# The value product of an attention stage issued in two parts, with its split into two float32r halves a step later

## The chip, the cores and the metric

One core of one Trainium2 chip runs the whole program. The metric is the device time of one execution in microseconds (us): 582.16 us for the kernel before, the median of three runs (581.98 to 582.57). The core has a matrix engine (TensorE, in the rows PE for its matmuls and PEld for its weight loads), a vector engine (VectorE, DVE), a scalar engine (ScalarE, ACT), a general one (GpSimd, POOL) and a queue that issues the DMAs (SyncE, SP). Each works through its own instructions in order and waits on semaphores for the others.

## The reference

A causal attention over 2 batches, 12 heads, 448 tokens and a head size of 64; its output, laid out as 896 tokens by 768, goes through two gated layers, all in float32.

```python
scores = where(causal mask, -1e9, q @ k.T / 8)
attn   = exp(scores - rowmax);  attn = attn / (rowsum + 1e-9)
x = (attn @ v), heads side by side             # 896 x 768
h = x @ w_in;  g = h * cos(h);  x = g @ w_out  # 2048 wide
out = ((x @ w_a) * (x @ w_b)) @ w_o2           # 1536 wide
```

## The kernel before

The kernel has an attention stage (the first 88 us) and four matrix products after it (`h`, `y`, `b` and `a`, `o` in the rows). The products run as float32r matmuls of 448 columns, each operand split into a high and a low half (`hi`, `lo`), three matmuls for one. The weights are unpacked and split on the fly: a chunk is loaded to `w_raw`, scaled on ACT (line 100), shifted, packed and signed on DVE (lines 105, 111, 118), and split on ACT or POOL (lines 129, 131, 138).

Attention works on pairs of heads, 12 in all (n = 0 to 11), four steps to a pair, 48 steps. The seven query blocks of 64 rows of a pair have score rows of 64 to 448 columns, packed into four PSUM banks (`BANKS`): {448}, {320, 192}, {384, 64}, {256, 128}; step 4n+b treats bank b. In each step the loop at line 515 goes through the table `CYCLE` and calls every function whose offset fits, so that the instructions stand on each engine in the order of the table, step by step. An entry with offset k belongs to pair n at step 4n+k. For one pair that means:

- `scores` (PE, line 339, tile `s`): 64x64 array tiles, every second step, two steps ahead, into four `s` banks in rotation. A bank can be refilled once `row_max` has read it.
- `row_max` (DVE, line 362, writes `p` and `mn`): mask, scale and row minimum; every step.
- `exps` (ACT, line 384): the exponentials and their row sums; every step.
- `recip` (DVE, lines 391 and 392, tile `sums`): steps 2 and 4. `scale_p` (POOL, line 399): steps 3 and 5.
- `transposes` (PE, line 413, tile `pt`): 7 full-array transposes at steps 5 and 7, into two `t` banks. `keep` (line 424 on ACT, 426 on DVE, tile `pp`): copies them to SBUF at steps 6 and 8, and so frees the banks.
- `values` (PE, line 440, tile `xa`): step 10, 14 matmuls (28 records, as a float32 matmul takes two passes) with 128x64 array tiles, of 384, 256, 128 and 64 columns.
- `x_hi` (ACT, line 450) at step 12 and `x_lo` (DVE, line 455) at step 13: the split of the result.

In the first four steps a dummy matmul (`warm`, line 460) follows each entry of `values` in the table. The weights of the first matrix product are treated in between by the table `ASIDE`: one chunk's scale at step 20, shift at 22, pack at 24, sign at 26, split on POOL at 28; the next ones from steps 32 and 46. From step 44 pieces of three matmuls of the product `h` are put in at the ends of steps.

Of the kernel before, what the change touches and what calls it, by code (L numbers as in the profile page):

```python
# [26 lines left out]
def tile_causal_attention_cos_gate_bilinear(  # L27
# [35 lines left out]
    def act_tiles(pool, tag, kind, b, n):  # L63
        return [
            tuple(pool.tile([P, S], F32R, tag=f"{tag}{b}_{t}{part}", name=f"{kind}{b}_{t}{part}") for part in ("hi", "lo"))
            for t in range(n)
        ]
# [89 lines left out]
    x = [act_tiles(xy, "xy", "x", b, NPAIR) for b in range(B)]  # L157
# [5 lines left out]
    def bank(tag, name):  # L163
        return psum.tile([P, 512], F32, tag=tag, name=name, bufs=BUFS[tag])

    def product(kind, f, acts, name, release, parts=1):

        ps = bank(next(cycle), name)[:, :S]
        n = len(acts)
        t = j = 0  # L170
        while t < n:
            hi, lo, k = chunks[kind, f, j]
            terms = [(hi, c, part) for c in range(k) for part in range(2)] + [(lo, c, 0) for c in range(k)]
            for i, (w, c, part) in enumerate(terms):
                nc.tensor.matmul(  # L175
                    ps,
                    w[:, c * P : (c + 1) * P],
                    acts[t + c][part],
                    start=t == 0 and i == 0,
                    stop=t + k == n and i == len(terms) - 1,  # L180
                )
                if (i + 1) % (len(terms) // parts) == 0 and i + 1 < len(terms):
                    yield ps
            t += k
            if release:
                del chunks[kind, f, j]
            if kind != "in":
                w_pump()
            j += 1
        yield ps  # L190
# [58 lines left out]
    NSTEP = NB * NP  # L249
# [10 lines left out]
    P_OFF, o = {}, 0  # L260
# [18 lines left out]
    with ExitStack() as actx:  # L279
        att = actx.enter_context(tc.tile_pool(name="att", bufs=2))  # L280
        T = {}
# [27 lines left out]
        @pairs  # L309
        def load_qk(n):  # L310
            b, i = divmod(n, NPAIR)
            T["raw", n] = t = att.tile([P, QK], F32, tag="qk_raw", name="qk_raw", bufs=4)
            cuts = (0, S + 2 * D, QK) if n == 0 else (0, QK)
            for c, d in zip(cuts, cuts[1:]):
                nc.sync.dma_start(out=t[:, c:d], in_=qk[b, i, :, c:d])

        @pairs
        def load_v(n):
            b, i = divmod(n, NPAIR)
            T["v", n] = t = att.tile([P, NJ, 2, D], F32, tag="v", name="v", bufs=4)  # L320
            nc.sync.dma_start(out=t, in_=v[b, i])

        @steps
        def scores(i):

            n, b = divmod(i, NB)
            if b % 2:
                return
            t = T["raw", n]
            for c in range(2):  # L330
                T["s", i + c] = bank("s", "s")
            for j in ORDER:
                c = 0 if j in BANKS[b] else 1
                if j not in BANKS[b + c]:
                    continue
                o = S_OFF[j]
                for e in range(2):
                    h, q = (slice(x * D, (x + 1) * D) for x in (e, SIDE[j][e]))
                    nc.tensor.matmul(  # L339
                        T["s", i + c][q, o : o + WIDTH[j]],  # L340
                        t[h, Q_COL[j] : Q_COL[j] + D],
                        t[h, FIRST[j] : FIRST[j] + WIDTH[j]],
                        start=True,
                        stop=True,
                    )
# [80 lines left out]
                    nc.vector.tensor_copy(dst, src)  # L426

        @pairs
        def values(n):

            T["xa", n] = ps = bank("x", "xa")
            pp, t = T["pp", n], T["v", n]

            parts = [(k, o, 6, pp[:, a:b]) for k, o, a, b in ((0, 0, 0, 3), (1, 2, 3, 5), (2, 4, 5, 6))]
            parts += [(3 + j // 2, TOKENS[j], TOKENS[j] + 1, pp[:, 6, j // 4]) for j in range(0, NJ, 2)]
            for k, o, w, p in parts:
                for e in range(2):
                    side = e if k < 3 else SIDE[2 * k - 6][e]
                    q = slice(side * D, (side + 1) * D)
                    nc.tensor.matmul(  # L440
                        ps[e * D : (e + 1) * D, o * D : w * D],
                        t[:, k, e],
                        p[:, :, :, q].rearrange("p s l q -> p (s l) q") if k < 3 else p[:, q],
                        start=k == 0,
                        stop=k == 6,
                    )
# [10 lines left out]
        def warm_up(n):  # L457
            ps = bank("x", "warm")
            for _ in range(n):
                nc.tensor.matmul(ps[:, :P], zeros, zeros, start=True, stop=True)  # L460
# [3 lines left out]
        def at(fn, i):  # L464

            n, b = divmod(i, NB)
            return i if fn in PER_STEP else n if b == 0 else -1
# [9 lines left out]
            (exps, 0),  # L477
            (scale_p, 3, 0),
            (scale_p, 5, 1),
            (values, 10),  # L480
            (transposes, 5, 0),
            (transposes, 7, 1),
            (x_hi, 12),
            (x_lo, 13),
            (load_qk, -10),
            (load_v, -2),
        ]
# [20 lines left out]
        with tc.manual_schedule():  # L508
            warm_up(7)
            load_qk(0)  # L510
            load_qk(1)
            load_qk(2)
            load_v(0)
            scores(0)
            for i in range(NSTEP + 14):
                for fn, offset, *args in CYCLE:
                    fn(at(fn, i - offset), *args)
                    if fn is values and i < WARM:
                        warm_up(1)
                for step, fn, *args in ASIDE:  # L520
                    if step == i:
                        fn(*args)
# [3 lines left out]
    with tc.manual_schedule():  # L526
# [20 lines left out]
        for m in range(N_Y):  # L547
            for b in range(B):
                ps = next(product("out", m, g[b], "y", b == B - 1))
# [15 lines left out]
        for m in range(N_Y):  # L565
            for b in range(B):
                ps = next(product("o2", m, c[b], "o", b == B - 1))
                o = work.tile([P, S], F32, tag="r", name="o")
# [50 lines left out]
```

## Time and profile before

| | |
|---|---|
| median of three runs | 582.16 us (581.98 to 582.57) |
| the profiled execution | 582.6 us, its span 580.5 us |
| granted TensorE clock | 1.00 of full speed |
| PE busy | 573.0 us, 99% |
| DVE, ACT, POOL busy | 361.7, 267.2, 222.9 us |
| attention | to 87.98 us |
| products | 87.98 us to the end |

The profile is of one execution. Its busy time of PE is modelled, since matmuls overlap, so the starts of the matmuls say more than the busy share. `x28` in a row is the number of records that were merged into it, `64*64` the array tile, and a bracket at the end of a row tells how long the engine had been idle and what released it.

### The profile page before, as it was taken

Reading aid. Unit: us, or ns where it says so; the run is one execution under the profiler, and the core shown is the slowest. Engines: PE = TensorE matmul, PEld = TensorE weight load, DVE = VectorE, ACT = ScalarE, POOL = GpSimd, SP = SyncE. Lnnn points to the kernel's source line nnn. Section 1 sums busy time; section 2 is a strip of 40 time slices with the busy share of each in tenths; the row PEclk is TensorE's granted clock in tenths of the full one; section 3 lists DMA queues with packets and bytes.
Section 4 is the critical chain, followed back from the end, with each engine's and each line's share of the span. In section 5 each row is a group of like instructions: output and inputs, shape, how many; then the busy total and the mean of one; then the engine's idle time right before and its main releaser. Section 6 shows DMA issues by size and latency. Waiting matters only on the chain.

```text
span 580.5 us, 8729 instructions
## 1 busy us (share of the span) xinstructions
PE 573.0 (99%) x3310; PEld 513.3 (88%) x3310; DVE 361.7 (62%) x599; ACT 267.2 (46%) x531; POOL 222.9 (38%) x200
## 2 busy tenths in 40 slices
PE   8999999999999999999999999999999999999997
PEld 6666679999999999999999999999999999999996
DVE  5888947777777765554455666666666666655400
ACT  5978937777777733232224333333333333222100
POOL 4567753666666643232223322222222222322200
PEclk9999999999999999999999999999999999999999
DMA  8755211333332343423243333333333333444000
GB/s 310 255 172 213 89 55 55 109 110 109 110 109 92 108 129 109 145 92 108 91 163 110 110 108 110 108 110 109 110 108 110 110 109 110 140 141 140 33 32 33
DMA packets 15450, 67.80 MB, mean 117 GB/s; under 512 B 1712, under 2 KB 3376, under 8 KB 15408
## 3 DMA queue, kind: packets, MB, share of 16 engines
q1 hardware_dynamic: 15408, 67.25, 34.4%
q8 instruction: 26, 0.43, 0.3%
q14 instruction: 16, 0.13, 0.1%
HBM read 64.49 MB, written 2.75 MB: 116 GB/s over the span
## 4 chain that ended last, share of the span: by engine, by line
PE 92%; DVE 3%; ACT 3%; issue 1%; POOL 0%; DVEq 0%; POOLq 0%
PE h L175 20%; PE y L175 20%; PE o L175 15%; PE a L175 15%; PE b L175 15%; PE xa L440 3%; ACT p L384 2%; PE pt L413 2%; PE s L339 2%; DVE p L362 1%; DVE pp L426 1%; PE warm L460 1%; ACT pp L424 0%; DVE sums L391 0%; DVE w_raw L118 0%
## 5 line engine op out<-in xcount | busy, mean ns | idle before, releaser
L138 POOL TENSOR_TENSOR w_lo<-w_raw,w_hi 128x768 fp32r<-128x768 f32 (+1 forms) x70 | 128.9, 1841 | 264.5 <-ACT w_hi L131 193.8
L111 DVE SCALAR_TENSOR_TENSOR w_raw<-w_raw 128x768 int32<-128x768 int32 (+1 forms) x70 | 124.4, 1778 | 63.3 <-ACT w_raw L100 62.4
L131 ACT ACTIVATE w_hi<-w_raw 128x768 fp32r<-128x768 f32 (+1 forms) x67 | 60.0, 896 | 163.1 <-DVE w_raw L118 99.9
L118 DVE SCALAR_TENSOR_TENSOR w_raw<-w_raw 128x768 int32<-128x768 int32 (+1 forms) x70 | 66.2, 946 | 0.4
L100 ACT ACTIVATE w_raw<-w_raw 128x768 f32<-128x768 f32 (+1 forms) x70 | 61.7, 881 | 0.0
L399 POOL TENSOR_SCALAR p<-p,sums 128x448 f32<-128x448 f32 (+6 forms) x84 | 44.0, 545 | 27.4 <-DVE sums L392 14.5
L384 ACT ACTIVATE p<-p,mn 128x448 f32<-128x448 f32 (+6 forms) x84 | 41.8, 501 | 13.4 <-DVE mn L362 13.2
L105 DVE TENSOR_SCALAR w_raw<-w_raw 128x768 int32<-128x768 int32 (+1 forms) x70 | 42.5, 607 | 0.0
L215 DVE SCALAR_TENSOR_TENSOR r<-k,h 128x448 f32<-128x448 int32 x32 | 19.8, 617 | 26.0 <-ACT k L214 25.7
L362 DVE CUSTOM_DVE_ANT_0 p<-s,mask 128x448 f32<-128x448 f32 (+6 forms) x84 | 31.3, 416 | 4.8 <-PE s L339 4.8
L569 DVE COPY o<-o 128x448 f32<-128x448 f32 x12 | 7.5, 624 | 35.3 <-PE o L175 35.3
L339 PE MATMUL s<-qk_raw 64*64 64x448 f32 (+6 forms) x336 | 28.1, 405 | 0.4 <-DVE mn L362 0.4
L214 ACT ACTIVATE k<-h 128x448 int32<-128x448 f32 x32 | 17.2, 538 | 18.4 <-PE h L175 17.6
L413 PE MATMUL pt<-ident,p 128*128 128x128 f32 x168 | 23.7, 279 | 1.9 <-ACT pp L424 1.2
L339 PEld LDWEIGHTS s<-qk_raw 64*64 64x64 f32 x336 | 15.9, 137 | 10.7 <-issue 3.9
L561 DVE TENSOR_TENSOR c<-a,bs 128x448 f32<-128x448 f32 x24 | 15.0, 624 | 15.3 <-PE a L175 15.3
L440 PEld LDWEIGHTS xa<-pp,v 128*64 128x64 f32 x336 | 16.1, 137 | 9.4 <-issue 7.1
L440 PE MATMUL xa<-pp,v 128*64 128x64 f32 (+3 forms) x336 | 23.8, 293 | 0.0
L413 PEld LDWEIGHTS pt<-ident,p 128*128 128x128 f32 x168 | 18.2, 141 | 4.8 <-issue 1.3
L231 DVE SCALAR_TENSOR_TENSOR r<-r,h 128x448 f32<-128x448 f32 x32 | 19.5, 609 | 1.5 <-ACT r L226 1.5
L221 ACT ACTIVATE r<-r 128x448 f32<-128x448 f32 x32 | 18.3, 571 | 0.0
L226 ACT ACTIVATE r<-r 128x448 f32<-128x448 f32 x32 | 18.2, 570 | 0.0
(377 smaller groups left out, 1564.6 us busy)
## 6 DMA issues: line engine op xcount, KB each, us to landing
w_raw<-in_w_in SPq DMA_DIRECT2D x16, 768.0 KB, 4.4
w_raw<-in_w_out SPq DMA_DIRECT2D x12, 768.0 KB, 4.3
w_raw<-in_w_b SPq DMA_DIRECT2D x12, 768.0 KB, 4.3
w_raw<-in_w_a SPq DMA_DIRECT2D x12, 768.0 KB, 4.3
w_raw<-in_w_o SPq DMA_DIRECT2D x12, 768.0 KB, 4.3
v<-in_v SPq DMA_DIRECT2D x12, 448.0 KB, 5.8
qk_raw<-in_qk SPq DMA_DIRECT2D x11, 448.0 KB, 5.6
w_raw<-in_w_out SPq DMA_DIRECT2D x6, 512.0 KB, 3.8
```

Of the source, the lines that this page charges most:

```text
L100: nc.scalar.activation(high, high, ACTF.Copy, scale=2.0**-112)
L105: nc.vector.tensor_single_scalar(low, low, 29, op=ALU.logical_shift_right)
L111: nc.vector.scalar_tensor_tensor(out=low, in0=high, scalar=3, in1=low, op0=ALU.logical_shift_left, op1=ALU.bitwise_or)
L118: nc.vector.scalar_tensor_tensor(out=low, in0=high, scalar=SIGN, in1=low, op0=ALU.bitwise_and, op1=ALU.bitwise_or)
L131: nc.scalar.activation(pair[0][:, :n], src, ACTF.Copy)
L138: engine.tensor_tensor(out=lo[:, :n], in0=f32(raw.pop(i)[:, :, 0]), in1=f32(hi)[:, :n], op=ALU.subtract)
L175: nc.tensor.matmul(ps, w[:, c * P : (c + 1) * P], acts[t + c][part], start=t == 0 and i == 0, stop=t + k == n and i == len(terms) - 1,)
L339: nc.tensor.matmul(T["s", i + c][q, o : o + WIDTH[j]], t[h, Q_COL[j] : Q_COL[j] + D], t[h, FIRST[j] : FIRST[j] + WIDTH[j]], start=True, st ...
L384: nc.scalar.activation(t, t, ACTF.Exp, bias=T["mn", n][:, c], scale=-1.0, accum_out=row_sum(n, j))
L399: nc.gpsimd.tensor_scalar(out=t, in0=t, scalar1=row_sum(n, j), scalar2=1.0, op0=ALU.mult, op1=ALU.mult)
L413: nc.tensor.transpose(dst, p_bufs[n % N_P][:, o : o + P], ident)
L440: nc.tensor.matmul(ps[e * D : (e + 1) * D, o * D : w * D], t[:, k, e], p[:, :, :, q].rearrange("p s l q -> p (s l) q") if k < 3 else p[:, ...
```

## The change

`values` gets an argument. Its first call (offset 9) takes the bank and issues the first part, two matmuls of 384 columns that start the accumulation; its second call (offset 11) issues the twelve others. The split follows at offsets 13 and 14 in place of 12 and 13, and the loop has one step more. Since `values` now stands twice in the table, the line that adds a dummy matmul after it in the first four steps acts twice a step.

```diff
@@ values @@
-        def values(n):
+        def values(n, ends):
-            T["xa", n] = ps = bank("x", "xa")
-            pp, t = T["pp", n], T["v", n]
+            if not ends:
+                T["xa", n] = bank("x", "xa")
+            ps, pp, t = T["xa", n], T["pp", n], T["v", n]
...
-            for k, o, w, p in parts:
+            for k, o, w, p in parts[1:] if ends else parts[:1]:
@@ CYCLE @@
-            (values, 10),
+            (values, 9, False),
+            (values, 11, True),
             (transposes, 5, 0),
             (transposes, 7, 1),
-            (x_hi, 12),
-            (x_lo, 13),
+            (x_hi, 13),
+            (x_lo, 14),
@@ the loop @@
-            for i in range(NSTEP + 14):
+            for i in range(NSTEP + 15):
```

On PE, in the steps 9 to 11 of the loop, the kernel before has the transposes of pair 1 (`pt`), the scores of pair 3 (`s`) and then all values of pair 0 (`xa`):

```order
L413 MATMUL pt<-ident,p_116 128x2x64 x2
L413 MATMUL pt<-ident,p_116 128x128
L413 MATMUL pt<-ident,p_116 128x2x64
L413 MATMUL pt<-ident,p_116 128x128 x3
L339 MATMUL s<-qk_raw 64x448 x2
L339 MATMUL s<-qk_raw 64x320 x2
L339 MATMUL s<-qk_raw 64x192 x2
L440 MATMUL xa<-pp,v 64x384 x2
L440 MATMUL xa<-pp,v 64x256 x2
L440 MATMUL xa<-pp,v 64x128 x2
L440 MATMUL xa<-pp,v 64x64 x8
```

In the changed kernel the same stretch of PE reads:

```order
L441 MATMUL xa<-pp,v 64x384 x2
L413 MATMUL pt<-ident,p_116 128x2x64 x2
L413 MATMUL pt<-ident,p_116 128x128
L413 MATMUL pt<-ident,p_116 128x2x64
L413 MATMUL pt<-ident,p_116 128x128 x3
L339 MATMUL s<-qk_raw 64x448 x2
L339 MATMUL s<-qk_raw 64x320 x2
L339 MATMUL s<-qk_raw 64x192 x2
L441 MATMUL xa<-pp,v 64x256 x2
L441 MATMUL xa<-pp,v 64x128 x2
L441 MATMUL xa<-pp,v 64x64 x8
```

The two widest value matmuls moved from behind the scores to ahead of the transposes, so that `xa` is now one group in front of `pt` and one behind `s`.

On DVE, in the steps 25 and 26 (a step after the pack of the first weight chunk), the kernel before has the row maxima of banks 1 and 2 (line 362) with the split `x_3lo` between them:

```order
L362 ISA p_115,mn<-s,mask 128x320
L362 ISA mn 128x1
L362 ISA p_115,mn<-s,mask 128x192
L362 ISA mn 128x1
L455 TENSOR_TENSOR x_3lo<-xa,x_3hi 128x448
L362 ISA p_115,mn<-s,mask 128x384
L362 ISA mn 128x1
L362 ISA p_115,mn<-s,mask 128x64
L362 ISA mn 128x1
L391 TENSOR_SCALAR sums<-sums 128x3
L392 RECIPROCAL sums<-sums 128x3
L426 COPY pp<-pt 128x4x128
```

In the changed kernel:

```order
L362 ISA p_115,mn<-s,mask 128x320
L362 ISA mn 128x1
L362 ISA p_115,mn<-s,mask 128x192
L362 ISA mn 128x1
L362 ISA p_115,mn<-s,mask 128x384
L362 ISA mn 128x1
L362 ISA p_115,mn<-s,mask 128x64
L362 ISA mn 128x1
L391 TENSOR_SCALAR sums<-sums 128x3
L392 RECIPROCAL sums<-sums 128x3
L426 COPY pp<-pt 128x4x128
L456 TENSOR_TENSOR x_3lo<-xa,x_3hi 128x448
```

The split moved from ahead of the reciprocal of the sums to behind it and behind the copy of the transposes. On ACT `x_hi` moves alike, from ahead of the two exponentials of step 4n+1 to behind them. POOL and SP keep their order.

## Rows read from the trace of the kernel before

**Rows 1.** The page: PE's busy time, and the granted clock in 40 slices.
```profile
PE 573.0 (99%) x3310; PEld 513.3 (88%) x3310; DVE 361.7 (62%) x599; ACT 267.2 (46%) x531; POOL 222.9 (38%) x200
...
PEclk9999999999999999999999999999999999999999
```
**Rows 2.** The chain that ended last, two of its pieces: start, us, what.
```profile
87.98 109.03 PE h L175 x537
...
488.84 87.57 PE o L175 x432
```
**Rows 3.** Timeline, PE, 25 to 31 us: start, us, engine, line, operation, tile.
```profile
27.04 0.98 PE L413 MATMUL pt<-ident,p 128*128 128x128 f32 x7
27.95 1.09 PE L339 MATMUL s<-qk_raw 64*64 64x448 f32 x12
28.98 1.98 PE L440 MATMUL xa<-pp,v 128*64 128x384 f32 x28
30.89 0.33 PE L413 MATMUL pt<-ident,p 128*128 128x128 f32 x1
```
**Rows 4.** Timeline, weight loads of one value group, 28.9 to 29.8 us.
```profile
29.35 0.14 PEld L440 LDWEIGHTS xa<-pp,v 128*64 128x64 f32 x2 [0.18 <-issue]
29.68 0.14 PEld L440 LDWEIGHTS xa<-pp,v 128*64 128x64 f32 x2 [0.18 <-issue]
```
**Rows 5.** Timeline, PE, 71 to 72.6 us: transposes between matmuls of the product.
```profile
71.36 0.92 PE L413 MATMUL pt<-ident,p 128*128 128x128 f32 x7
72.04 0.45 PE L175 MATMUL h<-x_1lo,w_hi 128*128 128x448 f32 x1
72.32 0.36 PE L175 MATMUL h<-x_2hi,w_hi 128*128 128x448 f32 x1
```
**Rows 6.** Timeline, PE: the value groups of pairs 3 and 8.
```profile
34.65 1.98 PE L440 MATMUL xa<-pp,v 128*64 128x384 f32 x28
...
66.91 1.98 PE L440 MATMUL xa<-pp,v 128*64 128x384 f32 x28
```
**Rows 7.** Timeline, PE and PEld: where they waited for others, 40 to 59 us.
```profile
40.56 0.73 PEld L339 LDWEIGHTS s<-qk_raw 64*64 64x64 f32 x8 [1.01 <-DVE mn L362]
...
57.27 0.62 PEld L339 LDWEIGHTS s<-qk_raw 64*64 64x64 f32 x12 [0.88 <-DVE mn L362]
...
58.65 0.95 PE L413 MATMUL pt<-ident,p 128*128 128x128 f32 x7 [0.51 <-ACT pp L424]
```
**Rows 8.** Timeline, DVE and ACT around the split of pair 3.
```profile
40.43 0.61 DVE L455 TENSOR_TENSOR x_3lo<-xa,x_3hi 128x448 fp32r<-128x448 f32 x1
...
40.97 0.54 DVE L362 CUSTOM_DVE_ANT_0 p<-s,mask 128x384 f32<-128x384 f32 x1
...
41.17 0.19 ACT L384 ACTIVATION_READ_ACCUMULATOR p<-p,mn 128x1 f32 x1
...
41.59 0.16 DVE L391 TENSOR_SCALAR sums<-sums 128x3 f32<-128x3 f32 x1
```
**Rows 9.** Timeline, DVE: the same step of two other pairs.
```profile
35.07 0.17 DVE L391 TENSOR_SCALAR sums<-sums 128x3 f32<-128x3 f32 x1 [0.53 <-ACT p L384]
...
53.84 0.17 DVE L391 TENSOR_SCALAR sums<-sums 128x3 f32<-128x3 f32 x1 [0.57 <-ACT p L384]
```
**Rows 10.** Timeline, ACT and PE, 63 to 69 us: a copy, the transposes behind it, the next.
```profile
63.81 0.58 ACT L424 ACTIVATE pp<-pt 128x512 f32<-128x512 f32 x1
...
64.53 1.24 PE L413 MATMUL pt<-ident,p 128*128 128x128 f32 x7
...
68.82 0.98 PE L413 MATMUL pt<-ident,p 128*128 128x128 f32 x7
```
**Rows 11.** Timeline, PE at the start, and DVE at the end of the attention.
```profile
7.03 0.71 PE L460 MATMUL warm<-zeros 128*128 128x128 f32 x4
...
15.65 0.96 PE L413 MATMUL pt<-ident,p 128*128 128x128 f32 x7 [0.48 <-ACT pp L424]
...
88.60 0.62 DVE L455 TENSOR_TENSOR x_5lo<-xa,x_5hi 128x448 fp32r<-128x448 f32 x1 [4.78 <-ACT x_5hi L450]
```

## The prediction

> **What bounds the kernel now.** I read the page first, then the chain of waits, then the timeline of PE over the attention, and last DVE and ACT at the places where PE waits. The page says that PE is busy 99% of the span and that its clock is granted in full in all 40 slices [rows 1], so the clock is no term here. The chain shows that from 87.98 us on nothing but PE's product matmuls decides: `h` runs 109.03 us in 537 matmuls, 0.203 us each, and so on to the last product [rows 2]. So the attention is worth exactly the time at which PE leaves it, and every microsecond won or lost there goes straight into the end.
>
> In the attention a pair costs PE 5.67 us when it waits for nobody: of this the transposes take 0.91 (27.04 to 27.95), the scores of banks 0 and 1 take 1.03 (27.95 to 28.98), the values 1.91 (28.98 to 30.89) [rows 3]; the other transposes and scores take 0.91 each. From the value group of pair 3 to that of pair 8, PE needed 66.91 - 34.65 = 32.26 us for five pairs [rows 6], which is 3.91 us more than 5 x 5.67 = 28.35. That is the stretch in which DVE and ACT also prepare the first weights, and PE is seen waiting there for DVE's row maxima (1.01 and 0.88 us) and for ACT's copy of the transposes (0.51 us) [rows 7]. These 3.91 us are all that a better order could win.
>
> **The change part by part.** *One more regrouping of the array per pair.* The group of transposes costs 0.91 us between groups that use another array tile [rows 3]. Between matmuls of the product, which use the same full array, it costs 72.32 - 71.36 = 0.96 less one product step of 0.20, so 0.76 [rows 5]. The difference, 0.15 us, is what one change of array tile costs. Before, a pair has five such changes (transposes, scores, transposes, scores, values, and again). With the values in two groups, one between scores and transposes and one behind the next scores, it has six. So each of pairs 0 to 8 costs PE 0.15 us more, 1.4 in all. Pairs 9 to 11 have product pieces around them: their three value groups become six, six more changes, 0.9. Together +2.3 us, if nothing hides it. The bounds: from below 0, since the transposes between product matmuls lose nothing that way; from above 0.91 less 72.04 - 71.36 = 0.68, so 0.23, if the product's longer first step behind them (0.28) is not put down to them. Over 15 changes that is 0 to 3.5 us. I take 0.15, for it counts each group once.
>
> The Trainium skill states, in "TensorEngine Tiling (Array Packing)", section Key Properties, that changing the tiling mode, and not merely the tile, drains the engine. The trace agrees in kind, with the 0.15 us above, and the rule speaks against this change; no row shows what is drained.
>
> *The first part's length.* Its matmuls run from 28.98 to 29.68, 0.70 us; with a gap of some 0.10 behind it, an estimate from the 0.15, 0.80 us pass until the transposes [rows 3, 4]. The second part then takes 1.91 + 0.15 - 0.80 = 1.27.
>
> *Where the first part lands.* It is queued ahead of the transposes of step 4n+9, and both wait for the same ACT copy (the copy frees the `t` bank for the one and gives `pp` to the other). At 15.65 and 58.65 PE sits idle for just this copy [rows 7, 11]; the first part can't fill that wait, it stands behind it too, and the transposes come 0.80 us later. It can fill the waits for DVE's row maxima, 1.01 and 0.88 us, since those stand behind the transposes. If DVE kept its times, that alone would win some 0.8 us at each, 1.6 in all.
>
> *But DVE doesn't keep its times.* Before, `x_lo` stands ahead of the reciprocal of the sums, and so runs while ACT finishes the two exponentials on which the reciprocal waits. ACT's last reading for it ends at 41.17 + 0.19 = 41.36; the reciprocal's first instruction came at 41.59 only because DVE was busy, with the 0.54 us slot of `x_lo` (40.43 to 40.97) among its work [rows 8]. Without it DVE would be there at 41.59 - 0.54 = 41.05, and wait to 41.39: 0.34 us idle, and `x_lo` still to be done behind the copy. So a pair in which DVE is the bound loses 0.34. Where ACT's scale of a weight chunk is what releases the reciprocal, DVE was idle 0.53 and 0.57 already [rows 9], with `x_lo` done; there DVE's schedule becomes ACT's plus the whole 0.54 slot.
>
> Walking this down: at 35 us ACT is as late as PE (three changes, 0.47) less the 0.43 slot of the `x_hi` that left its place, +0.04, and DVE behind it +0.04 + 0.54 = +0.58. Pair 5 (rows 8) adds 0.34, so +0.92; the next one 0.35 by the same working, +1.27. At 53.84 ACT's release is late by 0.44, so DVE is at +0.98. The next pair adds about 0.2. So the row maxima, the exponentials and the ACT copy of 63.81 come about +1.2 us late, at 65.0. From there: 0.58 for the copy and 0.14 until PE starts (63.81 + 0.58 = 64.39 to 64.53) [rows 10], so the first part starts at 65.74; then 0.80 + 0.91 + 1.03 + 1.27 = 4.01 to the next transposes, at 69.75. Before they started at 68.82 [rows 10]: PE is +0.93 late there. Of the 1.4 us of changes up to that point about 0.5 went into waits, no more.
>
> *The end.* Behind that PE has work without a wait, and the six changes add 0.9: +1.8. As DVE is then later against PE than before, I allow 0.1 for the first part of pair 10, which again needs ACT's copy: +1.9 us.
>
> *Edits at nothing.* Four more dummy matmuls at the start: two take at most 0.71 us [rows 11], so the four cost up to some 0.9 us of PE, which PE then idles less before the copy that frees it at 15.65; without that cover they would cost these 0.9. The split a step later at the end: `x_lo` of the last pair came at 88.60 [rows 11] and the product needs it from the 11th matmul of the next unit on; behind the second part stand 12 matmuls of earlier units and ten more, 22 x 0.203 = 4.5 us, against about 1.4 for the copy and the subtraction. Nothing is late there; without this cover it would cost those 1.4. The loads of `v` wait for the second part, about a microsecond later; they are issued more than two pairs ahead of their use. The extra step holds only the last `x_lo`.
>
> *The sum.* The profiled execution took 582.6 us, span 580.5 and 2.1 around it: 582.6 + 1.9 = 584.5. The median of the runs is 0.4 below the profiled one, so 582.16 + 1.9 = **584.1 us**.
>
> **The rivals.** *The waits are covered (no measurable change).* DVE isn't later than before, for instance because the idle 0.34 us are taken up elsewhere; then the first part fills both waits for the row maxima: +2.3 - 1.6 = +0.7, 582.9. For it: the waits are there and the first part is long enough. Against it: nothing on DVE gets shorter, and in the rows `x_lo` did fill a hole.
>
> *The stretch speeds up (faster).* With the split out of the way, row maxima and exponentials run up to 0.54 us earlier within a pair, so that the scores come earlier and PE stops waiting in the whole stretch of weights: -3.91 + 2.3 = -1.6, 580.6. It decides from the point on at which more than 2.3 + 1.2 of the 3.91 go. Against it: the reciprocal still waits for the exponentials, and behind it the copy and the next maxima.
>
> *The changes cost nothing beyond the waits in the trace, but DVE is as late as I say.* Then PE only follows the copies: about +0.9 at 69.75 with a shorter second part, and +1.0 in the end, 583.1.
>
> *It is worse than I say.* Six pairs of 0.34 without any regain (2.0) and all of the 2.3 us: +3 to +4, 585 to 586.
>
> That the change doesn't do what it says isn't open: the order on PE and DVE is as listed.
>
> **How the numbers follow.** A measurement of this kernel tells about 0.2%, 1.2 us, from no change, so the bounds are 581.0 and 583.3. Chances: the forecast (583.3 to 585) 0.52, worse than that 0.08; waits covered, or changes that cost less, 0.26 together; the stretch speeds up 0.14. That gives slower 0.60, the same 0.26, faster 0.14. The range: at the upper end the forecast with changes at 0.23 us (3.5 less the 0.5 that goes into waits, plus 0.1), +3.1, 585.3; at the lower end half way into the faster rival, 581.4. The forecast's own range is 583.2 to 585.3.
>
> **What the next profile would show.** Before the weights, pairs at 5.82 us in place of 5.67, and transposes at 0.91 with a value group of 0.80 ahead of them. On DVE an idle time of 0.3 us ahead of the reciprocal of three sums, and `x_lo` behind the copy. PE's waits for row maxima shorter than 1.01 and 0.88 us, waits for the ACT copy longer. The last value group ending some 2.5 us later, 0.6 of it because one more product piece stands ahead of it. It would be wrong if the pairs before the weights stayed at 5.67, or if the copy that stood at 63.81 came at the same time or earlier.

## The result, and the profile after

The changed kernel took **585.4 us** (median of 5 runs, 584.84 to 585.46), against 582.16 before (5 runs, 581.98 to 582.58): a ratio of 1.0052, with a 95% interval of 1.0041 to 1.0062, which is 2.4 to 3.6 us slower. The forecast was 584.1 in a range of 581.4 to 585.3, so the direction was right and the move was larger than forecast (3.0 to 3.2 us for 1.9); the median lies 0.1 us above the end of the range, the time by the ratio (585.2) just inside it. The profiled execution took 584.84 us, of which 582.7 were span.

The page and the chain of the changed kernel answer to [rows 1, 2]:

```profile
PE 575.2 (99%) x3318; PEld 512.6 (88%) x3318; DVE 361.9 (62%) x599; ACT 268.0 (46%) x531; POOL 220.6 (38%) x200
```
```profile
90.83 108.42 PE h L175 x534
...
491.09 87.57 PE o L175 x432
```

PE has 8 records more and is still busy 99% of the span; the clock is granted in full (mean 0.999). As before, PE works without a stop from the end of the attention to the end of the program: the last product starts 2.25 us later (491.09 for 488.84) and is as long as it was. What the change costs, it costs ahead of 90 us.

One pair of the changed kernel where PE waits for nobody, from the timeline of PE (start, us, engine, line, operation, tile), answers to [rows 3]:

```profile
20.75 0.87 PE L441 MATMUL xa<-pp,v 128*64 128x384 f32 x4
21.55 0.99 PE L413 MATMUL pt<-ident,p 128*128 128x128 f32 x7
...
23.49 1.34 PE L441 MATMUL xa<-pp,v 128*64 128x256 f32 x24
24.75 0.99 PE L413 MATMUL pt<-ident,p 128*128 128x128 f32 x7
```

The first part takes 21.55 - 20.75 = 0.80 us and the second 24.75 - 23.49 = 1.26: both as worked out ahead.

The waits that answer to [rows 7], from the timelines of PE and of its weight loads:

```profile
40.38 0.73 PEld L339 LDWEIGHTS s<-qk_raw 64*64 64x64 f32 x8 [0.25 <-DVE mn L362]
...
58.73 0.63 PEld L339 LDWEIGHTS s<-qk_raw 64*64 64x64 f32 x12 [1.15 <-DVE mn L362]
```
```profile
60.02 0.87 PE L441 MATMUL xa<-pp,v 128*64 128x384 f32 x4 [0.42 <-ACT pp L424]
```

The first wait for row maxima fell from 1.01 to 0.25 us. The second didn't fall; it grew from 0.88 to 1.15. Between the two something made DVE late that wasn't in the sum.

DVE in the same steps, which answers to [rows 8, 9]:

```profile
34.34 0.17 DVE L391 TENSOR_SCALAR sums<-sums 128x3 f32<-128x3 f32 x1 [0.88 <-ACT p L384]
...
41.21 0.17 DVE L391 TENSOR_SCALAR sums<-sums 128x3 f32<-128x3 f32 x1 [0.26 <-ACT p L384]
...
42.09 0.62 DVE L456 TENSOR_TENSOR x_3lo<-xa,x_3hi 128x448 fp32r<-128x448 f32 x1
...
54.90 0.17 DVE L391 TENSOR_SCALAR sums<-sums 128x3 f32<-128x3 f32 x1 [0.79 <-ACT p L384]
```

The split now stands behind the reciprocal and its copy, and DVE is idle ahead of the sums: 0.26 us where it had no wait, 0.88 and 0.79 where it had 0.53 and 0.57. That also was forecast. The surprise stands four microseconds later. POOL and DVE at 45 us in the changed kernel, and the transposes of PE that follow:

```profile
44.00 0.91 POOL L129 TENSOR_SCALAR w_hi<-w_raw 128x768 fp32r<-128x768 f32 x1
...
44.99 1.85 POOL L138 TENSOR_TENSOR w_lo<-w_raw,w_hi 128x768 fp32r<-128x768 f32 x1
...
45.13 1.74 DVE L391 TENSOR_SCALAR sums<-sums 128x4 f32<-128x4 f32 x1 [0.30 <-ACT p L384]
...
46.90 0.18 DVE L392 RECIPROCAL sums<-sums 128x4 f32<-128x4 f32 x1
...
47.00 0.53 DVE L426 COPY pp<-pt 128x384 f32<-128x384 f32 x1
...
47.58 0.55 PE L413 MATMUL pt<-ident,p 128*128 128x128 f32 x3 [0.49 <-DVE pp L426]
```

And the same place in the kernel before:

```profile
44.38 0.91 POOL L129 TENSOR_SCALAR w_hi<-w_raw 128x768 fp32r<-128x768 f32 x1
...
44.99 0.32 DVE L391 TENSOR_SCALAR sums<-sums 128x4 f32<-128x4 f32 x1 [0.30 <-ACT p L384]
...
45.37 1.87 POOL L138 TENSOR_TENSOR w_lo<-w_raw,w_hi 128x768 fp32r<-128x768 f32 x1
```

An addition on four columns lasts 1.74 us in the changed kernel, where [rows 8, 9] have 0.16 and 0.17 for three. It starts 0.14 us after POOL's subtraction `w_lo` and ends at 46.87, when that subtraction ends (44.99 + 1.85 = 46.84). Before, it started 0.38 us ahead of that subtraction and was through. The only wait printed for it is that for ACT ahead of its start, none for POOL: the hold is inside the instruction's own duration. Behind it stand the copy that the transposes wait for, and the next row maxima.

### The profile page after: what moved, and what is told of

The parts are those of the page before. It is cut to its first block, busy times and chain, and to the rows that moved or that the text cites. A ratio compares the mean times of both kernels' runs of the same rounds, so it can differ in the third digit from the quotient of the medians.

```text
span 582.7 us, 8754 instructions
## 1 busy us (share of the span) xinstructions
PE 575.2 (99%) x3318; PEld 512.6 (88%) x3318; DVE 361.9 (62%) x599; ACT 268.0 (46%) x531; POOL 220.6 (38%) x200
## 4 chain that ended last, share of the span: by engine, by line
PE 92%; ACT 4%; DVE 3%; issue 1%; POOL 0%; ACTq 0%; POOLq 0%
PE h L175 20%; PE y L175 20%; PE o L175 15%; PE a L175 15%; PE b L175 15%; ACT p L384 3%; PE xa L441 3%; PE pt L413 2%; PE s L339 1%; DVE p L362 1%; DVE sums L391 1%; DVE pp L426 1%; PE warm L461 1%; ACT pp L424 0%; ACT w_raw L100 0%
## 5 line engine op out<-in xcount | busy, mean ns | idle before, releaser
L399 POOL TENSOR_SCALAR p<-p,sums 128x448 f32<-128x448 f32 (+6 forms) x84 | 41.3, 510 | 30.9 <-ACT pp L424 13.0
L441 PE MATMUL xa<-pp,v 128*64 128x64 f32 (+3 forms) x336 | 26.4, 297 | 1.5 <-ACT pp L424 1.4
L339 PE MATMUL s<-qk_raw 64*64 64x448 f32 (+6 forms) x336 | 26.7, 393 | 0.5 <-DVE mn L362 0.5
```

The source lines that it names most:

```text
L339: nc.tensor.matmul(T["s", i + c][q, o : o + WIDTH[j]], t[h, Q_COL[j] : Q_COL[j] + D], t[h, FIRST[j] : FIRST[j] + WIDTH[j]], start=True, st ...
L399: nc.gpsimd.tensor_scalar(out=t, in0=t, scalar1=row_sum(n, j), scalar2=1.0, op0=ALU.mult, op1=ALU.mult)
L441: nc.tensor.matmul(ps[e * D : (e + 1) * D, o * D : w * D], t[:, k, e], p[:, :, :, q].rearrange("p s l q -> p (s l) q") if k < 3 else p[:, ...
```

## The experiments

All ratios are against the kernel before, run in turn on the same chip (its medians there: 582.28 to 582.56 us), with 95% intervals; a ratio weighs all executions and so differs a little from the quotient of the medians. In the sums below, *PE's waits over six pairs* is read the same way each time: the time from the transposes at 30 to 31 us to those six pairs later, at 68 to 71 us, less six pairs of work (6 x 5.67 = 34.02 us with the values whole, 6 x 5.825 = 34.95 in two parts, where 5.82 and 5.83 were read). Before that gives 68.82 - 30.89 - 34.02 = 3.91 us of waits [rows 3, 10], and the changed kernel, by these two rows of PE's timeline,

```profile
30.58 0.99 PE L413 MATMUL pt<-ident,p 128*128 128x128 f32 x7
...
70.11 0.98 PE L413 MATMUL pt<-ident,p 128*128 128x128 f32 x7
```

39.53 - 34.95 = 4.58 us.

**The two halves of the change.** First the values in two parts alone, with the result split at its old steps:

```diff
-            (x_hi, 13),
-            (x_lo, 14),
+            (x_hi, 12),
+            (x_lo, 13),
```

> The values in two parts as in the changed kernel, but the split of the result at its old steps (12 and 13). Theory A (the cost has three parts: one more change of array tile per pair, 15 x 0.15 = 2.3 us; DVE held up because x_lo no longer fills the time before the reciprocal; and one collision at 45 us, where DVE's four-column addition waits out POOL's 1.85 us subtraction): without the late split DVE keeps its times, the first part fills PE's two waits for row maxima, and 2.3 - 1.6 = +0.7 us remain, 582.9; the addition at 45 us stays under 0.5 us. Rival B (the changes of array tile are all of it): no less than +2.3, 584.5 or more. Rival C (the split's place doesn't matter): as the changed kernel, +3.2, 585.4.

Measured: 582.66 us, ratio 1.0007 (0.9998 to 1.0016). The waits over six pairs, from its timeline of PE:

```profile
31.10 0.98 PE L413 MATMUL pt<-ident,p 128*128 128x128 f32 x7
...
68.54 0.99 PE L413 MATMUL pt<-ident,p 128*128 128x128 f32 x7
```

37.44 - 34.95 = 2.49 us, so 1.42 of the 3.91 are filled, where the prediction's rival "the waits are covered" had 1.6. The cut of the values alone costs little: 15 changes of array tile cost 2.3, the filled waits give 1.4 back, and 0.9 are left. The ratio has 0.4 us of them, with an interval from nothing to 0.9. In the profiled execution the last product starts at 489.52, 0.68 us later than before, and 0.87 later when counted from the copy at the start (15.46 for 15.65; why the starts differ is told further down).

Then the later split alone, with the values whole (from the kernel before):

```diff
-            (x_hi, 12),
-            (x_lo, 13),
+            (x_hi, 13),
+            (x_lo, 14),
...
-            for i in range(NSTEP + 14):
+            for i in range(NSTEP + 15):
```

> The values whole at step 10 as before, only the split of the result a step later (13 and 14). Theory A: no further change of array tile, but DVE idle about 0.3 us ahead of the reciprocal of three sums in each pair and late by up to 0.9 to 1.3 us in the stretch of weights (30 to 66 us), of which PE, which waits for it there, feels most: +0.8 to +1.3 us, 583.0 to 583.5; with the addition caught behind POOL's subtraction as well, up to +2. Rival B (the changes of array tile are all of it): no change, 582.2.

Measured: 583.87 us, ratio 1.0025 (1.0014 to 1.0035). It has the long addition too:

```profile
45.34 1.85 POOL L138 TENSOR_TENSOR w_lo<-w_raw,w_hi 128x768 fp32r<-128x768 f32 x1
...
45.47 1.74 DVE L391 TENSOR_SCALAR sums<-sums 128x4 f32<-128x4 f32 x1 [0.30 <-ACT p L384]
```
```profile
30.89 0.98 PE L413 MATMUL pt<-ident,p 128*128 128x128 f32 x7
...
70.59 0.98 PE L413 MATMUL pt<-ident,p 128*128 128x128 f32 x7
```

39.70 - 34.02 = 5.68 us of waits, 1.77 more than before. So the later split brings the hold, and the question was how much of the loss is the hold and how much the idle time ahead of the reciprocal.

**Without the additions.** Next the changed kernel, and the kernel before, without the addition of 1e-9 to the row sums, all 24 of them:

```diff
-            nc.vector.tensor_scalar_add(t, t, 1e-9)
```

> The changed kernel without the addition of 1e-9 to the row sums (in float32 it changes nothing in a sum of at least 1). Theory A: the addition, not the reciprocal behind it, is what waits 1.74 us for POOL at 45.13; without it the reciprocal takes its usual 0.18 there, DVE gains those 1.6 us at that place and 0.2 us at each of the other reciprocals, and PE gains 0.8 to 1.5 us: 583.9 to 584.6. Rival D (the reciprocal, or any DVE instruction over SBUF alone, waits for POOL just so): the reciprocal then shows some 1.7 us at that place and the kernel gains 0.3 us at most, 585.1.

> The kernel before without the addition of 1e-9. The control for the one above: here the addition waited 0.32, 0.38, 0.74 and 0.37 us at four places. Theory A: DVE gains 0.2 us at each reciprocal and up to 0.5 at those four, and PE gains part of this where it waits, 0.4 to 1.2 us: 581.0 to 581.8, less than the changed kernel gains by the same edit. Rival D: within 0.3 us of before.

Measured: the changed kernel 581.93 us, 0.9992 (0.9984 to 1.0001); the kernel before **579.97** us, 0.9953 (0.994 to 0.9965). Both gained more than expected, by 0.0060 and 0.0047 of the time, 3.5 and 2.7 us. So the additions cost something at other places than 45 us too: in the kernel before six of the 24 took 0.32 to 0.74 us in place of 0.17, each until an operation of POOL had ended. The rows of the kernel before without them, against [rows 10, 11]:

```profile
14.77 0.96 PE L412 MATMUL pt<-ident,p 128*128 128x128 f32 x7 [0.43 <-ACT pp L423]
...
66.19 0.98 PE L412 MATMUL pt<-ident,p 128*128 128x128 f32 x7
```

The transposes are ahead by 0.88 us at the start (15.65 to 14.77; 0.17 of this is an earlier start, as the first row maxima begin at 6.02 for 6.19) and by 2.63 at the end of the six pairs (68.82 to 66.19). Against each other the two kernels without additions differ by 0.9992 - 0.9953 = 0.0039 of the time, 2.3 us: with no addition held in either, the change still loses what its changes of array tile cost. This is the version that beats both kernels; in float32, an addition of 1e-9 to a sum that holds the row's largest exponential, 1, changes no bit.

The same with the values in two parts and the split at its old steps (from the changed kernel):

```diff
-            nc.vector.tensor_scalar_add(t, t, 1e-9)
...
-            (x_hi, 13),
-            (x_lo, 14),
+            (x_hi, 12),
+            (x_lo, 13),
```

> The values in two parts, the split at its old steps, and without the addition of 1e-9. Theory A: the two edits are independent where PE is bound by its own work; without the addition PE waits less in the stretch of weights, so the first part has less to fill and its 2.3 us of changes of array tile weigh more: 580.3 to 581.3, not better than the kernel before without the addition (580.0). Rival H (both gains add up): 579.9 or less.

Measured: 581.32 us, 0.9985 (0.9976 to 0.9994). Without the additions the cut of the values costs 0.9985 - 0.9953 = 0.0032 of the time, 1.9 us, where it cost 0.4 with them. PE has fewer waits by then, and the first part has less to fill: the waits over six pairs are 66.19 - 29.93 - 34.02 = 2.24 us with the values whole and 66.70 - 30.11 - 34.95 = 1.64 in two parts, so 0.60 of the 2.3 us of the changes come back in place of 1.42.

As these kernels differ from the change in 24 places, they show that the additions matter, but not that the one at 45 us does.

**The one addition.** So the four-column addition of pair 6 alone was left out, in the changed kernel, in the kernel before and in the later split alone:

```diff
-            nc.vector.tensor_scalar_add(t, t, 1e-9)
+            if (n, odd) != (6, 1):
+                nc.vector.tensor_scalar_add(t, t, 1e-9)
```

> The changed kernel without one single addition of 1e-9 (pair 6, the four sums of step 28, the one that took 1.74 us beside POOL's subtraction); the 23 others stay. Moving the subtraction a step later only let the next addition run into it, so this takes away the other party. Theory A (the collision costs PE what the walk from the rows did not have, about 0.8 us): the reciprocal takes 0.18 us at its place, the transposes of step 31 come 0.7 to 1.0 us earlier, no other addition takes over 0.6 us, and the kernel takes 584.2 to 584.8. Rival E (DVE's lateness is made up of something else, and PE meets the next wait): 585.1 or more.

> The control: the kernel before without the same single addition, which took 0.32 us there. Theory A: DVE gains 0.35 us at most at one place, PE 0 to 0.35: 581.9 to 582.5. If this kernel gained as much as the changed one, what is gained would not be the collision.

> Only the split a step later, and without the single addition of step 28 (which took 1.74 us in that kernel too). Theory A (the late split costs DVE its filled time, about 0.3 us a pair, and the collision besides): 0.3 to 1.0 us slower than before are left of its 1.5, 582.6 to 583.3. Rival I (with the values in one part, PE can bear DVE's lateness, and all of the late split's cost was the collision): within 0.2 us of before, 582.1 to 582.5.

Measured: the changed kernel 583.99 us, 1.0029 (1.0018 to 1.0039); the kernel before 582.31, 0.9997 (0.9989 to 1.0006); the later split alone 582.27, 1.0000 (0.9991 to 1.0009). One instruction of four columns is worth 0.0052 - 0.0029 = 0.0023 of the time, **1.3 us**, in the changed kernel, 0.0025 (1.5 us) in the later split alone, and nothing that can be measured in the kernel before, where it ran ahead of POOL's `w_lo`. In the changed kernel that is more than was expected (584.2 to 584.8), and for the later split alone it is rival I of its expectation, not theory A. POOL and DVE in the changed kernel without it:

```profile
45.12 1.85 POOL L138 TENSOR_TENSOR w_lo<-w_raw,w_hi 128x768 fp32r<-128x768 f32 x1
...
45.26 0.18 DVE L393 RECIPROCAL sums<-sums 128x4 f32<-128x4 f32 x1 [0.30 <-ACT p L384]
45.36 0.53 DVE L427 COPY pp<-pt 128x384 f32<-128x384 f32 x1
```

The reciprocal takes the addition's place, 0.14 us after POOL's start as well, and lasts 0.18 us; the copy behind it keeps its 0.53 while POOL runs until 46.97. So not every instruction of DVE is held there, but the addition is.

PE's rows of the changed kernel without it, and then of the later split without it:

```profile
30.67 0.98 PE L414 MATMUL pt<-ident,p 128*128 128x128 f32 x7
...
68.74 0.99 PE L414 MATMUL pt<-ident,p 128*128 128x128 f32 x7
```
```profile
30.11 0.99 PE L414 MATMUL pt<-ident,p 128*128 128x128 f32 x7
...
68.18 0.98 PE L414 MATMUL pt<-ident,p 128*128 128x128 f32 x7
```

The first has 38.07 - 34.95 = 3.12 us of waits, 1.46 less than with the addition; the second 38.07 - 34.02 = 4.05, 1.63 less, and 0.14 more than the kernel before. With the values whole, then, the idle time that the late split leaves on DVE costs nothing that can be measured; together with the two parts it takes back 3.12 - 2.49 = 0.63 of the 1.42 us that they fill.

**Moving the hold away.** POOL's first `w_lo` a step later:

```diff
-            (28, w_lo, 0, nc.gpsimd),
+            (29, w_lo, 0, nc.gpsimd),
```

> The changed kernel with POOL's subtraction of the first weight chunk (w_lo) one step later, behind the scaling of step 29, so that DVE's addition at 45.13 meets POOL idle or at the end of its 0.9 us copy. Theory A (the collision is a term of its own): the addition takes under 0.4 us in place of 1.74, the transposes of step 31 come 0.8 us earlier, and the kernel takes 584.2 to 584.8. Rival E (DVE is late anyway, the wait only takes the place of another): 585.1 to 585.5.

Measured: 585.24 us, 1.0054 (1.0041 to 1.0067), no better. The hold only moved to the next addition:

```profile
47.74 1.86 POOL L138 TENSOR_TENSOR w_lo<-w_raw,w_hi 128x768 fp32r<-128x768 f32 x1
...
47.94 1.69 DVE L391 TENSOR_SCALAR sums<-sums 128x3 f32<-128x3 f32 x1 [0.26 <-ACT p L384]
```

As a test of the cost it says nothing, since it didn't take the hold away; as a test of the mechanism it speaks for it: another addition, another time, and again 1.7 us, to POOL's end (47.74 + 1.86 = 49.60, and 47.94 + 1.69 = 49.63).

**Two side questions.** The four more dummies, taken out again:

```diff
-                    if fn is values and i < WARM:
+                    if fn is values and args[0] and i < WARM:
```

> The changed kernel with one dummy matmul a step in the first four steps, as before, in place of two. Theory A: the four more are hidden behind the copy that frees PE at 15 us: within 0.4 us of the changed kernel, 585.0 to 585.8. Rival F (they cost what they run, up to 0.9 us): 584.5.

Measured: 584.98 us, 1.0048 (1.0032 to 1.0063), inside the interval of the changed kernel, though the ratio alone couldn't exclude rival F. The traces can: from the first row maxima to the release by ACT's copy the changed kernel takes 14.92 - 5.57 = 9.35 us and this one 15.02 - 5.64 = 9.38. The dummies were hidden.

And the first part behind the transposes, so that it doesn't hold them up (with the split at its old steps):

```diff
-            (values, 9, False),
             (values, 11, True),
             (transposes, 5, 0),
             (transposes, 7, 1),
-            (x_hi, 13),
-            (x_lo, 14),
+            (values, 9, False),
+            (x_hi, 12),
+            (x_lo, 13),
```

> The values in two parts, the split at its old steps, and the first part queued behind the transposes of step 4n+9 in place of ahead of them. Six changes of array tile a pair, as with the first part ahead. Theory A: the transposes then come at once with ACT's copy, 0.8 us earlier for DVE's copy behind them, and the first part still fills the waits for row maxima: 0 to 0.6 us better than with the first part ahead (582.7), 582.1 to 582.7. Rival G (the place of the first part within its step decides): over 1 us better or worse.

Measured: 583.81 us, 1.0026 (1.0017 to 1.0036), worse than expected and worse than the same kernel with the first part ahead (1.0007). The place ahead of the transposes, which I had counted as a cost, isn't one. Its waits over six pairs:

```profile
30.37 0.98 PE L413 MATMUL pt<-ident,p 128*128 128x128 f32 x7
...
68.20 0.98 PE L413 MATMUL pt<-ident,p 128*128 128x128 f32 x7
```

37.83 - 34.95 = 2.88 us, so the first part fills 0.39 us less from this place. The last product says the same: it starts at 489.21, which, counted from the copy at the start (14.76), is 1.26 us later than before, for 0.87 with the first part ahead. The other 0.7 us between the two medians (583.81 and 582.66) are of the size by which executions differ at their start, and the two profiled executions, 582.97 and 583.3 us, stand the other way round for that reason. Why the first part fills less there stays open.

## Why the prediction was right in direction and too small

**What held.** The change of array tile: pairs of 5.82 and 5.83 us were read for the 5.82 forecast, and behind the waits the transposes at 70.11 are 1.29 us later than before and the last product 2.25, so 0.96 was added between them, for 0.9 + 0.1. The lengths of the two parts. DVE's idle time ahead of the reciprocal, 0.26 us read for 0.34. That the first part fills part of the waits and the later split takes some of it back. The dummies and the last `x_lo` hidden. With the one addition out, so with that hold gone, the sum comes out near: the ratio is 1.0029, a cost of 1.7 us, where 1.9 was forecast.

**What failed** is one step, "Walking this down": from 41 us on it carried DVE's lateness from pair to pair ("so +0.92; the next one 0.35 by the same working, +1.27"), with every instruction of DVE at the duration it had before. At 45 us one of them, the addition, met POOL's `w_lo` and took 1.74 us. That term was missing: by the waits 1.46 us of PE, by the ratios 1.3. With it, PE's waits in six pairs are 0.67 above before (4.58 - 3.91), not 0.5 below; the 2.3 us of changes and these 0.67 make 2.97, which is what was measured (3.0 by the ratio). The step "about 0.5 went into waits" was near without the hold (3.91 - 3.12 = 0.79), with both of its parts sized too large: the first part fills 1.42 us for 1.6, and DVE's lateness takes back 0.63 for 1.1.

It could have been read. In [rows 8] the addition of three columns takes 0.16 us; at 44.99 in the kernel before one of four columns takes 0.32, and ends as POOL's `w_hi` does (44.38 + 0.91 = 45.29, 44.99 + 0.32 = 45.31). Plainer still, later in the same kernel:

```profile
63.57 0.91 POOL L129 TENSOR_SCALAR w_hi<-w_raw 128x768 fp32r<-128x768 f32 x1
...
63.77 0.74 DVE L391 TENSOR_SCALAR sums<-sums 128x4 f32<-128x4 f32 x1
```

It ends at 64.51, 0.03 us after POOL. I took the duration as a property of the instruction, and not of what POOL did beside it. Once a chain on DVE is moved by 0.5 us against POOL's, those places had to be asked about. The Trainium skill states, in "SBUF — State Buffer", section Who interferes with whom, that VectorE and GpSimd share a pair of ports of the SBUF under an exclusive lock, which VectorE needs in some of its modes, and that the later one is stopped until the other's instruction has ended. The runs agree: 1.74 us beside an operation of 1.85. They show the hold and not the port. Which modes are held is seen here only by kind: the addition is, the reciprocal and the copy of `pt` aren't.

**Of the rivals,** "the waits are covered" is what the cut alone does (1.42 of 1.6 us, 582.66 for 582.9), and it failed for the whole change for the reason given: DVE does get later. "It is worse than I say" gave the right size, 585 to 586, by the wrong mechanism: no sum of 0.34 us losses, which without the hold cost nothing in the later split alone and 0.63 us in the change, but one instruction. "The changes cost nothing beyond the waits" fails on the pairs where PE waits for nobody, 5.82 and 5.83 us for 5.67. "The stretch speeds up" has nothing for it; no run of the change or of a part of it is under the kernel before by more than the measurement tells, unless the additions go as well.

**A start that isn't the change's.** The profiled execution of the changed kernel was 0.73 us ahead at 15 us (14.92 for 15.65). Its 28 first matmul records of scores took 1.83 us up to the next group's start, those of the profiled execution before 2.76 (4.27 to 7.03). This differs among executions of all the kernels: the later split alone, with and without the one addition of 45 us, has the same instructions up to there, and took 2.58 and 1.68 us for these records. So lateness was read against the copy of that place. It is also why the last product starts only 2.25 us later when the profiled executions are compared; counted from the copy it is 2.98.

The traces show what differs. These matmuls lie across the rise of TensorE's clock. In the kernel before, the records of the dummy matmuls ahead of them,

```profile
1.79 2.55 PE L460 MATMUL warm<-zeros 128*128 128x128 f32 x11
4.27 2.83 PE L339 MATMUL s<-qk_raw 64*64 64x448 f32 x28
7.03 0.71 PE L460 MATMUL warm<-zeros 128*128 128x128 f32 x4
```

start 0.21 us apart (1.79 to 3.92 for ten of them), those behind 0.11 (7.25, 7.36, 7.47): half the rate, and then the full one. The trace's record of the granted clock at full speed (2.4 GHz) begins at 6.53 us in this execution, at 4.65 in that of the changed kernel, and at 6.17 and 4.34 in the two of the later split. The later it begins, the longer the 28 records take.

At the place that the prediction named for its check, the ACT copy of 63.81 stands at

```profile
65.47 0.58 ACT L424 ACTIVATE pp<-pt 128x512 f32<-128x512 f32 x1
```

1.66 us later, and 2.39 later counted from the start's copy, for +1.2 forecast. In the changed kernel without the one addition it stands at 64.13, 0.94 later by the same count (15.03 at the start), so the hold accounts for the difference.

## What to carry to other kernels

When a change shifts the work of one engine against another's, look not only at who waits for whom but at which instructions will now run beside each other: read in the trace whether an instruction's duration is the same everywhere, and where it isn't, what ran beside the long ones and whether both ended together. A tiny instruction on VectorE between two others that matter, beside microsecond-long GpSimd work, is worth a trial without it: here the 24 additions together were worth more (0.47% of the kernel before) than the 1.6 us that the most hopeful rival gave the new order, though the one of 45 us alone was worth nothing there. And price a reordering by its own fixed cost (0.15 us for each further group on the array) against the waits that are in the trace, since what it can win ends with them.

## What the runs showed of the hardware

A `tensor_scalar` of DVE on 128x3 or 128x4 float32 values takes 0.16 to 0.17 us alone and 1.69 to 1.75 us when it starts 0.13 to 0.20 us after a POOL subtraction of 1.85 us; it ends with it, and the trace shows no wait for POOL. A reciprocal of the same size at the same place took 0.18 us, a copy of 128x384 out of PSUM 0.53. The hold comes from the order of the starts: 0.38 us ahead of that subtraction the addition took 0.32 (held by POOL's `w_hi`), 0.14 behind it 1.74, so half a microsecond of DVE against POOL became two.

The first 28 matmul records of scores take 1.67 to 2.76 us from one profiled execution to another. They follow 14 records of dummy matmuls, the first at 0.99 us, and the record of the clock at full speed begins at 3.99 us in the execution with the shortest time and at 6.53 in that with the longest. The mean granted clock of 0.998 to 1.0 that is listed for these executions doesn't show this: it is 1.00 from 0 to 4 us too, where the dummies start 0.21 us apart.
